# DeltaNet and GELU MLP on one core: beta laid out in its order of use, early loads on two queues, weights that wait for no load, and a new order for every engine

## The chip, the cores and the metric

The kernel runs on one core of one Trainium2 chip. The core has five engines that run side by side: TensorE (PE, with its weight loads as PEld) multiplies matrices, VectorE (DVE), ScalarE (ACT) and GpSimd (POOL) work on tiles, and SyncE (SP) issues transfers. Each runs its own list of instructions in the order in which they stand; semaphores make one wait for another. Transfers between device memory and on-chip memory are issued by SP, ACT and POOL and carried by 16 DMA engines. Products land in PSUM, which has eight banks, and are copied out by ACT or DVE. The metric is the time of one execution on the device, in microseconds.

## The reference

Each of 4 x 8 heads keeps a 48 x 48 state and reads 768 tokens in order; the outputs of all heads then go through a dense layer, a GELU and a second dense layer.

```python
k_n = k / (np.linalg.norm(k, axis=-1, keepdims=True) + 1e-06)
for t in range(S):                                  # S = 768
    kt, vt, bt = (k_n[:, :, t].copy(), v[:, :, t].copy(), beta[:, :, t, None].copy())
    y[:, :, t] = np.einsum('bhd,bhde->bhe', q[:, :, t], state)
    v_old = np.einsum('bhde,bhd->bhe', state, kt)
    state = state + bt[:, :, :, None] * np.einsum('bhd,bhe->bhde', kt, vt - v_old)
...
x = np.ascontiguousarray(attn_out.transpose(0, 2, 1, 3)).reshape(B * S, H * D)   # 3072 x 384
h = x @ w_in                                        # 384 x 2048
g = 0.5 * h * (1.0 + np.tanh(c * (h + 0.044715 * h * h * h)))
return (g @ w_out).astype(np.float32)               # 2048 x 384
```

## The kernel before

The 768 tokens are taken in 12 chunks of 64 (`c`); a chunk has two units (`u = 2c + x`) of 16 heads each. Within a chunk the recurrence is turned into products: a triangular system per head is inverted, and one state goes from chunk to chunk.

The code only declares operations (`A(...)`): the engines on which each may run, what it reads and writes, its PSUM bank. The text table `ORDER` then fixes everything: each word names an operation, its engine (`:a` ACT, `:d` DVE, `:g` POOL, `:s` SP, none for TensorE) and, for products, its bank (`@4`). Every engine runs its words in the order of the table, and `Flow.emit` derives the semaphore waits from what is read and written. Where an operation has alternatives (transposing on TensorE or by DMA, one instruction or two), the table's words choose.

The steps that matter here, with the names used in the table:

- `k0x1.10`, `q2.01`, `v1.00`: loads of a quarter of a chunk's k, q or v (96 KB; chunk 0's k in halves of 48 KB). They stand on SP; chunk 0's k may also stand on ACT. Three chunks' buffers rotate.
- `beta..`: beta is loaded, transposed on TensorE (`betaT`), negated out of PSUM into `bsb` (`betaN`), split into a high and a low part (`betaH`, `betaL`) and spread over rows (`betaS`, `betaC`). Before the change this is done twice, for chunk 0 and for chunks 1 to 11, and all 32 rows are loaded twice, once for each half of a tile.
- `sq`, `sum`, `pow`, `eps`, `inv`: square, sum and root that give 1/norm of k. `kn` (or `knc` for both units) scales k with it; `qb`/`qbc` and `vb`/`vbc` cast q and v.
- `Tk`, `Tq` or `T` transpose a unit's k and q on TensorE, with the evictions `kTk`, `kTq`, `kT`; `turn` does it by a DMA on SP. `GD`, `GQ` or `G` are the products of keys with keys and queries, `dn` and `wq` their evictions (`wqa` with `wqb` on POOL in place of `wq`).
- `F`, `lp`, `x0`, `L`, then `xm1`/`xa1` to `xm6`/`xa6` on DVE, then `xb`: the leaf, which solves blocks of 8 tokens, for a whole chunk. `xe`/`xec` spread its result; `KZ`, `kz`, `GM`, `lw` build the triangular system.
- `X10`/`X11`, `A4`, `rt4`, `B4`, `bde4.` (or `xi4` and `bdc4.`), `A5`, `rt5`, `B5`, `be5.`: the inversion.
- `V`, `K`, `R`, `U`, `Un`, `S`, `Sn`, `Q`, `O`, `On`: the chain over chunks; `On` gives the chunk's output `xo`. `X` with `xT` (TensorE) or `turnx` (DMA) transposes it.
- `up0` to `up15` with `gelu0` to `gelu3`, `down..` with `Z` and `out`: the MLP of a chunk. Its weights come by four loads on POOL: `w1.0`, `w1.1`, `w2.0`, `w2.1`. Before the change `w1.` waits for chunk 1's k and `w2.` for chunk 0's v.
- `fill`: a product of a zero tile with itself into a bank that nobody reads. 140 are declared; the table holds as many as it likes, two before the change.

Of the kernel before, what the change touches and what calls it, by code (L numbers as in the profile page):

```python
# [21 lines left out]
muq1:g ladj4.0:a k2.01:s betaN011:d pow.1:a betaN110:d eps.1:g pad3:d k2.11:s inv.1:d triwq1:d betaN010:d low1:d kn.2:d v0.10:s kn.3:d qb.1:a Tk.2@7
v0.01:s qb.0:g Tk.3@5 kTk.2:d q2.01:s rows1:g Tq.1@4 sq.0a:a betaN111:d kTk.1:d q2.10:s kTq.1:d kTk.3:a sum.0a:d q2.00:s GD.3@4 betaH1:d pow.0a:a
Tq.0@7 sq.2:a eps.0a:d rpad0:g v1.00:s inv.0a:d GD.2@2 betaN000:d GD.1@0 dn.3:a kn.0:g betaL1:d q1.01:s betaH0:d betaS1@6 dn.2:a sum.2:d low2:g
q1.00:s dn.1:a Tk.0@4 first0:d F.1@2 kTq.0:d pow.2:a q1.10:s eps.2:g kTk.0:d trilw2:g q1.11:s GQ.1@0 lp.1:d GD.0@4 betaL0:d x0.1:d L.1@7 q3.01:s
dn.0:a two:d inv.2:d GQ.0@2 wz:d knc.2:g xm1.1:d qbc.2:a F.0@4 k3.00:s wq.0:d xa1.1:d q3.10:s betaS0@5 xm2.1:d xa2.1:d betaS3@2 w1.0:g lp.0:d k3.11:s
betaC0:a xm3.1:d ladj5.1:d L.0@3 triwq2:a ladj4.1:d T.5@4 v0.00:s x0.0:d wqa.1:a xm1.0:d first1:g xa1.0:d kT.5:a qb.3:g xa3.1:d xm2.0:d v0.11:s
xa2.0:d trilw3:g Tq.3@0 xm4.1:d xm3.0:d betaC1:a xa3.0:d qb.2:g xa4.1:d xm5.1:d xm4.0:d T.4@6 xa4.0:d xa5.1:d betaS2@1 xm5.0:d xm6.1:d kT.4:a xa6.1:d
xa5.0:d Tq.2@4 kTq.3:d xb.1:g xm6.0:d triwq5:g xa6.0:d betaC2:a xb.0:d G.5@6 w1.1:g kTq.2:a xe.1:d G.4@0 dn.4:a v2.11:s xe.0:d KZ.1@4 kz.1:a wq.4:d
mwp1:g dn.5:a GM.1@4 xec.1:d KZ.0@0 ladj5.0:a F.2@3 wqa.5:a betaC3:a lw.1:d kz.0:a lp.2:d bdz1:d L.2@3 k3.01:s GM.0@4 x0.2:d X10.1:g KZ.2@6 lw.0:d  # L30
KZ.3@0 kz.3:a X11.1:g kz.2:a xm1.2:d GM.3@0 xa1.2:d rpad1:g A4.1@2 X11.0:g lw.3:d X10.0:g rt4.1:d k3.10:s xm2.2:d A4.0@1 X11.3:g xa2.2:d v1.01:s
B4.1@2 xm3.2:d xa3.2:d rt4.0:d q3.11:s GQ.2@6 GM.2@4 vb.0:a xm4.2:d vb.1:g wq.2:d k4.11:s B4.0@1 bde40.1:a triwq3:g lw.2:d V.0@6 X10.3:g k4.01:s
bde41.1:a bde40.0:a k4.00:s wqb.1:g xa4.2:d A4.3@2 xm5.2:d bde41.0:a A5.1@0 k4.10:s rt4.3:d GQ.3@4 R.0:a rt5.1:d A5.0@1 X11.2:g B4.3@2 v1.10:s rt5.0:d
B5.1@0 bde40.3:a xa5.2:d q3.00:s B5.0@7 X10.2:g xm6.2:d fill115@1 xa6.2:d be50.1:d be50.0:a v1.11:s wq.3:d xb.2:g be51.1:a A4.2@3 sq.3:a w2.0:g
# [224 lines left out]
def bass_deltanet__then__act_gelu_tanh_kernel(  # L259
# [24 lines left out]
    with nc.allow_non_contiguous_dma("strided loads"), nc.allow_low_precision("bf16 pipeline"):  # L284
# [619 lines left out]
```

## Time and profile before

| | us |
|---|---|
| median of 3 runs | 253.88 |
| lowest and highest run | 253.4, 254.34 |
| span of the profiled execution, which is its own time | 254.7 |
| PE busy | 226.0 (89%) |
| DVE busy | 185.8 (73%) |
| ACT busy | 157.4 (62%) |
| POOL busy | 130.1 (51%) |
| moved by DMA | 28.25 MB, mean 111 GB/s |

The page has the busy time of each engine over the span and in 40 slices, and then the chain of work that ended last. A row of the timeline gives start, length, engine, line, operation and tiles, with the count of instructions that were merged, and in brackets the idle time before it and what ended it. Rows of groups give busy time and the mean of one in ns. `PEclk` or "granted clock" is the TensorE clock as a share of full speed. L472 is a load of k, q or v, L824 an up product, L835 a down product.

### The profile page before, as it was taken

The page shows a single profiled execution, that of the slowest core. Times are in us where ns is not written, and L with a number is a line of the kernel's source. Part 1 is how long each engine was busy: PE and PEld are TensorE (multiplying, and loading weights), DVE is VectorE, ACT ScalarE, POOL GpSimd, SP SyncE. Part 2 cuts the span into 40 slices and gives each one's busy share as a digit, 9 for nine tenths or more (in the row PEclk, how much of TensorE's full clock was granted, in tenths as well). Part 3 has the DMA queues.
Part 4 walks back from the last instruction along what each step waited for, and adds up shares of the span by engine and source line. Part 5 has one row for each costly group of instructions (what it writes and reads, how often), then busy time and mean ns, then how long its engine had stood idle before and what let it go on. Part 6 is the DMA issues. An engine that isn't in the chain of part 4 may idle for free.

```text
span 254.7 us, 12256 instructions
## 1 busy us (share of the span) xinstructions
PE 226.0 (89%) x5500; PEld 178.3 (70%) x5502; DVE 185.8 (73%) x445; ACT 157.4 (62%) x244; POOL 130.1 (51%) x159
## 2 busy tenths in 40 slices
PE   0259558899999998999999899999999999999994
PEld 0148347687877877777778778787786778678672
DVE  6599989955996989898888779898494665755100
ACT  2637747949568888967647577743866534436261
POOL 7647448347563397627358968472535525330000
PEclk9999956689999999999999999999999999999999
DMA  5986995987785679789678517787359320332042
GB/s 103 165 144 118 184 162 95 165 127 117 128 130 105 112 126 124 135 165 147 119 146 167 100 36 131 147 153 130 56 93 167 62 49 4 33 68 64 3 93 62
DMA packets 104532, 28.25 MB, mean 111 GB/s; under 512 B 98592, under 2 KB 103712, under 8 KB 104480
## 3 DMA queue, kind: packets, MB, share of 16 engines
q1 hardware_dynamic: 99200, 23.79, 54.0%
q0 software_dynamic: 2880, 3.15, 7.8%
q8 instruction: 43, 0.70, 1.2%
q10 hardware_dynamic: 2400, 0.54, 1.1%
q14 instruction: 9, 0.07, 0.1%
HBM read 20.64 MB, written 4.72 MB: 100 GB/s over the span
## 4 chain that ended last, share of the span: by engine, by line
PE 73%; DVE 15%; ACT 4%; DMA 2%; ACTq 2%; issue 2%; SPq 1%; POOL 0%
PE ps L835 24%; PE ps L824 22%; PE ps L692 5%; PE ps L620 3%; PE ps L752 3%; PE ps L773 2%; DMA vraw<-in_v_dram 2%; PE ps L697 2%; PE ps L564 2%; DVE lw L623 2%; DVE xl L658 2%; PE ps L633 2%; PE ps L759 2%; DVE ps L655 2%; PE ps L609 1%
## 5 line engine op out<-in xcount | busy, mean ns | idle before, releaser
L824 PE MATMUL ps<-xT,W 128*128 128x256 bf16 x576 | 76.8, 277 | 0.4 <-DVE xl L658 0.4
L835 PE MATMUL ps<-W,gT 128*128 128x384 bf16 x384 | 72.7, 326 | 0.0
L828 ACT ACTIVATE gT<-ps 128x1024 bf16<-128x1024 f32 x48 | 48.4, 1022 | 26.4 <-PE ps L824 25.8
L824 PEld LDWEIGHTS ps<-xT,W 128*128 128x128 bf16 x576 | 52.2, 99 | 9.3 <-DVE xl L658 0.5
L835 PEld LDWEIGHTS ps<-W,gT 128*128 128x128 bf16 x384 | 34.0, 97 | 18.2
L682 POOL TENSOR_SCALAR_AFFINE_SELECT bd<-lw 64x512 bf16<-64x512 bf16 x34 | 22.6, 667 | 37.7 <-DVE lw L623 28.6
L704 DVE TENSOR_TENSOR rl<-ps,two 128x384 bf16<-128x384 f32 (+1 forms) x48 | 22.9, 484 | 9.7 <-PE ps L692 9.5
L623 DVE CAST_PREDICATED lw<-mlw,ps 128x832 bf16<-128x832 uint16 x24 | 24.3, 1018 | 6.8 <-PE ps L620 6.5
L499 POOL TENSOR_TENSOR nrm<-nrm,half 128x16 f32<-128x16 f32 x9 | 26.6, 2956 | 2.8 <-DVE nrm L497 2.7
L343 ACT ACTIVATE bd<-ps 32x256 bf16<-32x256 f32 (+1 forms) x40 | 16.8, 428 | 8.2 <-PE ps L692 4.4
L692 PEld LDWEIGHTS ps<-lw,bd 128*128 128x128 bf16 x384 | 15.5, 98 | 4.2 <-POOL bd L682 1.2
L692 PE MATMUL ps<-lw,bd 128*128 128x32 bf16 (+1 forms) x384 | 17.2, 183 | 1.2 <-POOL bd L682 1.1
L658 DVE TENSOR_TENSOR xl<-ps,xl 128x96 bf16<-128x96 f32 (+4 forms) x72 | 16.0, 228 | 2.0
L655 DVE TENSOR_TENSOR ps<-ps,xl 128x64 f32<-128x64 f32 (+5 forms) x72 | 15.6, 221 | 2.0 <-PE ps L649 0.5
L343 ACT ACTIVATE ob<-ps 128x384 f32<-128x384 f32 x17 | 8.3, 490 | 14.0 <-PE ps L835 14.0
L722 POOL COPY bd<-xi 64x256 f32<-64x256 f32 x20 | 8.0, 401 | 16.4 <-ACT xi L343 8.5
L540 PE MATMUL ps<-ident,tok 128*128 128x128 bf16 x80 | 7.8, 246 | 8.1 <-POOL tok L531 3.8
L531 POOL TENSOR_TENSOR tok<-kraw,nrm 128x384 bf16<-128x384 f32 x9 | 8.5, 945 | 12.7 <-DVE bsb L349 5.6
L349 ACT ACTIVATE kT<-ps 128x512 bf16<-128x512 f32 x18 | 10.4, 596 | 6.4 <-PE ps L609 6.4
L343 ACT ACTIVATE dn<-ps 128x512 bf16<-128x512 f32 x18 | 10.4, 593 | 5.3 <-PE ps L564 5.3
L620 PE MATMUL ps<-kT 48*64 48x56 bf16 (+1 forms) x768 | 11.1, 196 | 2.8 <-ACT kT L349 1.4
L599 POOL TENSOR_TENSOR zt<-xb,blk 128x2048 bf16<-128x2048 bf16 x3 | 10.9, 3642 | 4.1 <-DVE xb L669 3.9
(132 smaller groups left out, 428.3 us busy)
## 6 DMA issues: line engine op xcount, KB each, us to landing
qraw<-in_q_dram SPq DMA_DIRECT2D x48, 96.0 KB, 3.6
vraw<-in_v_dram SPq DMA_DIRECT2D x48, 96.0 KB, 3.5
kraw<-in_k_dram SPq DMA_DIRECT2D x44, 96.0 KB, 3.6
out_dram<-ob SPq DMA_DIRECT2D x22, 192.0 KB, 3.0
W<-in_moe_w_in_dram POOLq DMA_DIRECT2D x2, 768.0 KB, 8.8
W<-in_moe_w_out_dram POOLq DMA_DIRECT2D x2, 768.0 KB, 9.6
kraw<-in_k_dram ACTq DMA_DIRECT2D x7, 48.0 KB, 3.3
out_dram<-ob SPq DMA_DIRECT2D x3, 96.0 KB, 2.2
```

Of the source, the lines that this page charges most:

```text
L343: return e.activation(out, in_, ACT.Copy) if e is nc.scalar else e.tensor_copy(out, in_)
L499: if e is nc.scalar else e.tensor_tensor(nr[:, 1, hx], nr[:, 0, hx], half[:, hx], ALU.pow), reads=[nrn, "half"] + ["one"] * (c < ROOTS),
L620: ins = e.matmul(P(ps("GM"))[hf(a), o_ + c0:o_ + c1], kT[s][r, y, g, hf(a)], kT[s][r, z, g, C * a + c0:C * a + c1])
L623: A(("dve",), op("lw"), lambda e, P: e.copy_predicated(lw[m][:, :, 0:LW - LB], mlw[:, :, :].rearrange("p w t -> p (w t)")[:, 16:16 + LW - ...
L655: A(("dve",), f"xm{m}.{c}", lambda e, P, m=m, w=w, part=part: e.tensor_tensor(part(P), P(f"L.{c}")[:, off[m]:off[m] + 2 * H * w].rearrange ...
L658: A(("dve",), f"xa{m}.{c}", lambda e, P, m=m, part=part: e.tensor_tensor(xl[y][:, :, m + 1:LB], part(P), xl[y][:, :, m + 1:LB], ALU.add), ...
L682: A(("pool", "dve"), op(f"X1{a}"), lambda e, P, src=lw[m][hf(a), :, LW - C:LW], dst=bd[b_][hf(a), :, hf(a)], a=a: e.affine_select(out=dst, ...
L692: ins = e.matmul(P(name)[:, C * h + c0:C * h + c1], bd[b_][:, h, :], rhs[:, h, :])
L704: A(("dve",), op(f"rt{i}"), lambda e, P, i=i, c0=c0, c1=c1, r_=r_: e.tensor_tensor(r_[:, 0:H, c0:c1], P(ps(f"A{i}")).rearrange("p (h t) -> ...
L824: ins = e.matmul(P(ph)[:, 256 * f:256 * f + 256].rearrange("p (x t) -> p x t", x=2), W1[:, j, 128 * (i + f):128 * (i + f) + 128], x_[:, :, ...
L828: A(("act",), f"gelu{i // 4}.{c}", lambda e, P, i=i, ph=ph: e.activation(g_[:, i:i + 4, :], P(ph).rearrange("p (f t) -> p f t", f=4), ACT. ...
L835: ins = e.matmul(P(po)[:, 0:DM], g_[:, f, 128 * b:128 * b + 128], W2[:, f, :], start=(f == 0), stop=(f == FC - 1))
```

## The change

Beta's loads now write 16 rows, in the order in which the heads are used, in four loads of 24 KB; one set of transposes serves all chunks, `betaN` is two instructions, `betaH` and `betaL` one each, and `betaS` three groups of four chunks. The loads of chunks 0 to 2 may stand on SP or ACT. The weights' loads read no other load's buffer any more. And the whole table `ORDER` is a new one: 153 operations change engine, four units' transposes (`T.6`, `T.10`, `T.15`, `T.18`) and three chunks' (`X.1`, `X.2`, `X.11`) become DMA transposes, the inversion's `xi4`/`bdc4.` form goes out for `bde4.` everywhere, and 36 zero products stand in it, 16 of them ahead of `betaT` and all ahead of the first up product.

```diff
 ORDER = """
-bdz3:d tmplz:g k0x1.10:a k1.01:s tmpl0:g tmpl1:g bdz5:d k0x1.00:a beta11:s blk1:g one:g pad2:g pad0:d pad5:d ident:g trilw0:d beta01:s beta10:a bdz4:d
...
+k1.01:s pad5:g tmplz:g k0x1.01:a pad3:g tmpl0:g mmlw:g bdz1:g tmpl1:g k0x1.10:s rowz:g ident:d half:d bdz2:d one:d blk1:d identf:d wz:d fill20@0
+fill79@7 fill6@0 fill90@0 fill46@0 ident2:g fill30@0 fill78@2 fill44@0 fill109@0 k0x1.11:a ladj4.1:d k0x1.00:a bdz0:d bdz3:d triwq5:d unit:d blk2:g
...
-        braw = sb("braw", [32, NC, 2, C], F32)
+        braw = sb("braw", [2 * H, NC, 2, C], F32)
...
-            bv = beta.rearrange("b h s -> (b h) s").rearrange("r (c t) -> r c t", t=C)
-            for z, c0, c1 in (("0", 0, 1), ("1", 1, NC)):
+            bv = beta.rearrange("b h s -> (b h) s").rearrange("(m r y) (c t) -> m y r c t", m=2, y=2, t=C)
+            for a in range(2):
                 for y in range(2):
-                    A(("sp", "act"), f"beta{z}{y}", lambda e, P, y=y, c0=c0, c1=c1: e.dma_start(braw[:, c0:c1, y, :], bv[:, c0:c1, :]),
-                      writes=[f"braw{z}{y}"], dma=f"beta{z}{y}")
+                    A(("sp", "act"), f"beta{a}{y}", lambda e, P, a=a, y=y: e.dma_start(
+                        braw[H * y:H * y + H, :, a, :],
+                        bv[a ^ y, y]), writes=["braw"], dma="beta")
...
+            A(PE, "betaT", trans, reads=["braw", "identf"], alloc=("psb", 1), mode="f", mm=2 * NC)
+            for y in range(2):
+                A(("dve",), f"betaN{y}", lambda e, P, y=y: neg(
+                    e, bsb[:, :, :].rearrange("p c (x y g) -> p (c x) y g", x=2, y=2)[:, :, y, :],
+                    P("psb")[:, 0:2 * H * NC].rearrange("p (c y x g) -> p c y x g", y=2, x=2, g=4)[:, :, y, :, :]), writes=[f"bsb{y}"], frees=["psb"])
...
-                            A(("sp", "act") if c == 0 and n == "k" else SP, f"{n}{c}" + ("" if x is None else f"x{x}") + f".{a}{y}",
+                            A(("sp", "act") if c < 3 else SP, f"{n}{c}" + ("" if x is None else f"x{x}") + f".{a}{y}",
...
                 A(("pool",), f"w1.{i}", lambda e, P, f0=f0: e.dma_start(W1[:, :, f0:f0 + FF // 2], w1v[:, :, f0:f0 + FF // 2]),
-                  reads=["kraw10", "kraw11"], writes=[f"W1{i}"], dma=f"w1{i}")
+                  writes=[f"W1{i}"], dma=f"w1{i}")
                 A(("pool",), f"w2.{i}", lambda e, P, n0=n0: e.dma_start(W2[:, n0:n0 + FC // 2, :], w2v[:, n0:n0 + FC // 2, :]),
-                  reads=["vraw00", "vraw01"], writes=[f"W2{i}"], dma=f"w2{i}")
+                  writes=[f"W2{i}"], dma=f"w2{i}")
...
-              reads=[f"xl{y}", f"xl0{y}", f"bc_{0 if c == 0 else 1 if c < 4 else 2 if c < 8 else 3}"], writes=[f"xb{y}"])
+              reads=[f"xl{y}", f"xl0{y}", f"bc_{c // 4}"], writes=[f"xb{y}"])
```

ACT's list at the start of the program, before (`kraw` is a load of k, `braw` of beta, `one` the operation that loads the root's table, `sq` the square of k):

```order
L472 DMA kraw<-in_k_dram 64x4x48 x2
L432 DMA braw<-in_beta_dram 32x11x64
L472 DMA kraw<-in_k_dram 64x4x48
L432 DMA braw<-in_beta_dram 32x64
L472 DMA kraw<-in_k_dram 64x4x48
L343 ACT_TABLE_LOAD
L343 ACTIVATE lw<-tmpl 128x896
L472 DMA kraw<-in_k_dram 64x4x48
L366 ACT_TABLE_LOAD
L366 ACTIVATE one<-one 128x1
L495 ACTIVATE sq<-kraw 128x384
```

And after:

```order
L470 DMA kraw<-in_k_dram 64x4x48 x3
L470 DMA kraw<-in_k_dram 64x8x48 x3
L433 DMA braw<-in_beta_dram 8x12x64
L470 DMA kraw<-in_k_dram 64x8x48
L433 DMA braw<-in_beta_dram 8x12x64
L367 ACT_TABLE_LOAD
L367 ACTIVATE one<-one 128x1
L496 ACTIVATE nrm<-nrm 128x8
L496 ACTIVATE nrm<-nrm 128x16
```

ACT issues nine loads in place of five ahead of its table, the first squares and the copy of the template have gone from it (they stand on DVE and POOL), and one table load is left.

POOL's list around the first load of weights (`W`), before; the `kraw`, `nrm` row is a scaling of k, `xb` the leaf's result:

```order
L531 TENSOR_TENSOR tok<-kraw,nrm 128x8x48
L397 AFFINE_SELECT low<-low 128x1
L501 TENSOR_SCALAR nrm<-nrm 128x16
L411 COPY lw<-tmpl 128x448
L524 TENSOR_TENSOR tok<-kraw,nrm 128x2x8x48
L481 DMA W<-in_moe_w_in_dram 128x3x1024
L400 CAST xl<-unit 128x16
```

And after:

```order
L391 TENSOR_TENSOR own<-blk 128x64
L373 AFFINE_SELECT mlw<-mlw 64x64
L479 DMA W<-in_moe_w_in_dram 128x3x1024
L370 MEMSET muq 128x64
L392 TENSOR_TENSOR sel<-ident,own 128x1024
L412 COPY lw<-tmpl 128x448
L412 COPY wq<-tmpl 128x256
L375 AFFINE_SELECT mlw<-mlw 64x64
L529 TENSOR_TENSOR tok<-kraw,nrm 128x8x48
L383 AFFINE_SELECT rows<-rows 128x1024
L481 DMA W<-in_moe_w_out_dram 128x8x384
L522 TENSOR_TENSOR tok<-kraw,nrm 128x2x8x48
```

The first load of weights now stands ahead of every scaling of k on POOL, and a second one (`w2.1`) ahead of chunk 2's; `sel` has come from DVE to POOL.

TensorE's list in chunk 1 before, with the transposes of the output `xo` between products of the chain (L752, L773) and of the MLP (L824, L835):

```order
L697 MATMUL ps<-bd,rl_1 128x64 x8
L807 MATMUL ps<-ident,xo 128x128 x6
L752 MATMUL ps<-st,kT 64x48 x32
L835 MATMUL ps<-W,gT 128x384 x8
L824 MATMUL ps<-xT,W 128x256 x9
L773 MATMUL ps<-rs,bd 128x48 x16
```

And what stands in SP's list for it after:

```order
L470 DMA kraw<-in_k_dram 64x8x48
L809 DMA_TRANSPOSE xT<-xo 128x6x128
L470 DMA kraw<-in_k_dram 64x8x48
L551 DMA_TRANSPOSE kT<-tok 128x8x128 x4
L844 DMA out_dram<-ob 64x2x384
```

The six products have left TensorE, and the transpose stands on SP among the loads of later chunks, with the transposes of four units' k and q behind it.

More of the change, by code (lines that the diff above doesn't have):

```diff
@@ L22 @@
[L22 to L29, printed above, removed]
@@ new lines, in load_beta, with trans @@
+                    A(("sp", "act"), f"beta{a}{y}", lambda e, P, a=a, y=y: e.dma_start(
+                        braw[H * y:H * y + H, :, a, :],
+                        bv[a ^ y, y]), writes=["braw"], dma="beta")
+            def trans(e, P):
+                for c in range(NC):
+                    ins = e.transpose(P("psb")[:, 2 * H * c:2 * H * c + 2 * H], braw[:, c, :, :].rearrange("r x t -> r (x t)"), identf[:, :])
+                return ins
+            A(PE, "betaT", trans, reads=["braw", "identf"], alloc=("psb", 1), mode="f", mm=2 * NC)
```

212 lines of the change are left out of this document (103 added, 109 removed).

## The prediction

> **What bounds the kernel now.** I read the page first, then the busy time by stretches, then the chain of waits, then the timeline of the stretch that the chain leaves to engines other than TensorE. The stretches (core's time, length, busy time and count of PE, PEld, DVE, ACT, POOL, granted clock, DMA share, GB/s):
>
> ```profile
> 0.00:10.00 10.00, 1.46 (x12) 1.35 (x12) 5.19 (x15) 4.54 (x7) 7.05 (x26) 1.00 0.71 125
> 10.00:20.00 10.00, 4.74 (x90) 3.80 (x91) 9.01 (x24) 4.87 (x11) 5.11 (x9) 1.00 0.86 152
> 20.00:30.00 10.00, 7.19 (x181) 5.92 (x179) 9.59 (x42) 6.95 (x13) 6.50 (x11) 1.00 0.79 138
> 40.00:50.00 10.00, 8.10 (x260) 7.16 (x260) 9.82 (x21) 8.79 (x15) 5.51 (x8) 0.67 0.92 139
> 60.00:240.00 180.00, 177.32 (x4491) 138.91 (x4488) 136.66 (x313) 115.47 (x176) 94.97 (x93) 1.00 0.60 105
> ```
>
> Two stages show. From 60 to 240 us TensorE has work in 177.3 of 180 us, at full clock, with VectorE at 76% and the DMA engines at 60%: products set the pace, and only fewer products or an earlier start can shorten it. In the first 50 us VectorE is the full one (9.0 to 9.8 of 10) and TensorE waits. That opening ends where the first product with the MLP's weights starts:
>
> ```profile
> 8.46 0.51 ACT L495 ACTIVATE sq<-kraw 128x384 f32<-128x384 f32 x1
> 10.56 0.95 DVE L497 TENSOR_REDUCE nrm<-sq 128x16 f32<-128x768 f32 x1 [0.30 <-ACT sq L495]
> 22.14 0.24 DVE L655 TENSOR_TENSOR ps<-ps,xl 128x96 f32<-128x96 f32 x1
> 29.13 0.29 DVE L669 TENSOR_TENSOR xb<-xl,bc 128x128 bf16<-128x128 bf16 x1
> 46.67 0.81 ACT L343 ACTIVATE xo<-ps 128x768 bf16<-128x768 f32 x1
> 49.94 3.81 PE L824 MATMUL ps<-xT,W 128*128 128x256 bf16 x18
> ```
>
> So: norms start at 8.46, the leaf solves at 22.14, xb of chunk 0 is done at 29.4, its output xo at 47.5, and the first up product starts at 49.9. The rest takes 254.7 - 49.9 = 204.8 us. The sum is made against the profiled execution's 254.7 us; the runs' median of 253.88 lies 0.8 under it, which comes off at the end.
>
> **Term 1: norms to xb of chunk 0.** The rows that the work there is priced by:
>
> ```profile
> 13.06 1.96 DVE L531 TENSOR_TENSOR tok<-kraw,nrm 128x384 bf16<-128x384 f32 x1
> 14.95 0.54 DVE L531 TENSOR_TENSOR tok<-kraw,nrm 128x384 bf16<-128x384 f32 x1
> 12.63 2.05 POOL L382 TENSOR_SCALAR_AFFINE_SELECT rows<-rows 128x1024 bf16<-128x1024 bf16 x1
> 9.00 0.55 DVE L497 TENSOR_REDUCE nrm<-sq 128x8 f32<-128x384 f32 x1 [1.40 <-ACT sq L495]
> 9.70 0.83 ACT L495 ACTIVATE sq<-kraw 128x768 f32<-128x768 f32 x1
> L421 DVE MEMSET bd<- 128x512 f32 x4 | 1.9, 485 | 1.1 <-PEq L889 1.0
> 4.80 1.28 ACT L343 ACT_TABLE_LOAD   x1 [4.80 <-issue]
> 0.80 1.39 ACTq L472 DMA_DIRECT2D kraw<-in_k_dram  x2
> kraw<-in_k_dram ACTq DMA_DIRECT2D x7, 48.0 KB, 3.3
> ```
>
> Before, the first square stands on ACT behind a table load, a copy and a second table load, until 8.46. Now it stands on DVE, and its last piece of k is ACT's third issue: 0.80 + 3 x 0.70 = 2.9, and 3.3 more to land, 6.2. DVE has three memsets of 0.49 and a dozen shorter operations before that, some 4.6 us by my count from its start at 1, so it is free in time. Then DVE's own list: square 0.5 (as ACT's 0.51), copy 0.5, sums 0.55 and 0.95, the square of chunk 1's k 0.9 (as ACT's 0.83): 9.6. ACT has issued nine loads by 0.8 + 9 x 0.66 = 6.7 and loaded its table by 8.2, so the roots cost 0.3; four small operations 0.8, two scalings 2 x 0.54: 11.8. Chunk 0's first half: sum 0.55, copies and roots 1.5, scaling 0.54: 14.4. Then 0.3 + 0.95 + 0.28 for beta's high part, chunk 2's sum and lp, 1.1 for x0 and small ones: 17.0. Fewer beta copies (2 for 8, of 0.1 to 0.25 each) are in this.
>
> The leaf: from 22.14 to 29.1 DVE did 24 steps and 2.4 us of other work between, so the steps take 4.5; now they have 0.8 among them: 22.3, and with xb 0.3 22.6, against 29.4. That is 6.8 us earlier if nothing waits. Against it: the 1.96 row is the same scaling that takes 0.54 in the next, and it lies almost wholly beside POOL's 2.05 us select, so POOL's work can hold DVE up. POOL now has sel near those scalings and rows1 near betaL; I take one such stop, 1.4, off: 5.4 us earlier. Bounds: 6.8 and, with three stops, 2.6. One new wait stands in ACT's list: the square of chunk 2's k waits for its fourth load with five evictions and a root queued behind it, and DVE's sum and lp behind those. That load is SP's eleventh, out by 0.8 + 11 x 0.67 = 8.2 and 3.6 later landed (row below), 11.8; ACT gets there near 12.4, so 0.6 us covers it.
>
> **Term 2: xb to the first up product.** 46.67 + 0.81 - 29.42 = 18.1 us from xb to xo. In the new order ACT is the longest list here: 12 evictions of kT, wq, bd or bc, 4 of the short corner kind, 2 scaled ones, 6 wide ones.
>
> ```profile
> L349 ACT ACTIVATE kT<-ps 128x512 bf16<-128x512 f32 x18 | 10.4, 596 | 6.4 <-PE ps L609 6.4
> L343 ACT ACTIVATE bd<-ps 32x256 bf16<-32x256 f32 (+1 forms) x40 | 16.8, 428 | 8.2 <-PE ps L692 4.4 <-PE ps L697 3.1
> L346 ACT ACTIVATE bd<-ps,low 128x512 bf16<-128x512 f32 x8 | 5.4, 672 | 0.0
> L343 ACT ACTIVATE us<-ps 128x768 bf16<-128x768 f32 x10 | 8.1, 809 | 3.2 <-PE ps L773 3.1
> ```
>
> 12 x 0.596 + 4 x 0.428 + 2 x 0.672 + 6 x 0.81 = 15.1, plus 1.1 from xb to its first eviction: 16.2, or 1.9 earlier when ACT never waits. I take 0.9, bounds 1.9 and -1. The 36 zero products (2 before) all stand ahead of the first up product; 16 of them ahead of beta's transposes. A product of 512 columns is priced from 384 columns below, 5.21 / 32 = 0.163, so 0.22, and 0.43 where the clock is half: the 16 take 6.9 us from some 3 us on, and nothing on PE is due before 11.8. The 20 others cost 4.4 to 8.6 if nothing covered them; most stand behind a product that waits for an eviction of 0.6 anyway, and I take 0.3 (bounds 0 and 4.4).
>
> ```profile
> 245.98 5.21 PE ps L835 x32
> 241.07 4.91 PE ps L824 x45
> 50.01 3.74 PE ps L824 x18
> 33.00:43.00 10.00, 7.53 (x255) 6.78 (x256) 8.97 (x24) 5.20 (x10) 7.29 (x12) 0.50 0.68 117
> 46.50:53.00 6.50, 6.09 (x133) 4.87 (x120) 5.05 (x8) 5.61 (x9) 3.56 (x2) 0.51 1.26 190
> ```
>
> **Term 3: the weights' loads.** They now wait for no load: w1.0 stands on POOL behind some 7 us of templates (19 operations of 0.1 to 0.65), w2.1 behind rows1, near 17 us, both by my count. Before, w1.0 went out at 23.45. What a load of weights does to its neighbours:
>
> ```profile
> kraw<-in_k_dram SPq DMA_DIRECT2D x44, 96.0 KB, 3.6
> 23.45 1.01 POOL L481 DMA_DIRECT2D W<-in_moe_w_in_dram  x1
> 25.57 2.83 SPq L472 DMA_DIRECT2D kraw<-in_k_dram  x1
> 29.16 2.57 SPq L472 DMA_DIRECT2D qraw<-in_q_dram  x1
> W<-in_moe_w_in_dram POOLq DMA_DIRECT2D x2, 768.0 KB, 8.8
> 6.00:8.00 2.00, 1.42 (x12) 1.29 (x12) 0.62 (x4) 1.97 (x3) 1.93 (x7) 1.00 0.96 165
> 190.51 4.84 DMA vraw<-in_v_dram
> ```
>
> While w1.0 moved, SP's issue, else 0.64 to 0.68, took 2.83 and 2.57: three loads in 6.2 us, where nine fit, so some 4.1 us lost for all behind it. SP's 29th load (the last of chunk 1's q) would go out at 0.8 + 29 x 0.67 = 20; with two loads of weights ahead 28, landed at 32. ACT casts that q near 26.5, and POOL the v of chunk 0 near 25. So up to 5 us of waiting; with w2.1 coming too late to matter, 1. I take 2.5, since w2.1 moves for about half the time that matters. Also the gain of two queues is small: the share is 0.96 at 165 GB/s at 6 us, with SP alone on most of it. [...]
>
> Opening: 5.4 + 0.9 - 0.3 - 2.5 = 3.5 us earlier. Up starts at 46.4.
>
> **Term 4: products removed.** Four units' transposes (T, 8 products each) and three chunks' (X, 6 each) go to SP's queue; all of them stand after up's start in the order before.
>
> ```profile
> 79.44 0.45 PE ps L540 x8
> 55.79 2.46 SPq L553 DMA_TRANSPOSE kT<-tok  x1
> ```
>
> 4 x 0.45 + 3 x 6 x 0.056 = 2.8 us less on the engine that sets the pace. Their evictions go too, off the path. SP carries 29 transposes for 22, each 1.2 to 2.5 us of issue; queued behind a waiting transpose are loads of q, k and v for two chunks on. Everything else after up's start is the same products in another order, with DVE, ACT and POOL lists no longer than before: 0, bounds -3 (all of the 2.7 idle in 60 to 240 recovered) and +6 (one more detour like the 4.84 above, where the chain leaves PE for a late v).
>
> Sum: 254.7 - 3.5 - 2.8 = 248.4; less 0.8: **247.6**, say 247.5.
>
> **Rivals.** (a) The opening does better: no load waits and no port stops, the zero products keep the clock up, so that the half clock at 46.5 to 53 goes too. 18 up products took 3.74 there and take 18 x 4.91 / 45 = 1.96: 1.8 us. 6.8 + 1.9 + 1.8 + 2.8 off: 241.4 - 0.8 = 240.6. For it: the leaf's end at 22.6 rests on measured steps. Against it: only eight zero products stand between the first KZ and up, so TensorE stays as sparse there as at 33 to 43, where the clock was half. [...] (b) The change does not bring the opening forward, since the loads, not the order, set it: only term 4 stays, 251.1. (c) Both first loads of weights stand fully in the path: -5.0 and a second late load of 4.1 against 6.0: up starts 3.1 later, 254.7 + 3.1 - 2.8 - 0.8 = 254.2, no change. (d) Slower: SP's queue, with seven more transposes that wait, delivers v or q late in the product stage. Each such wait costs 4.84 by the one row above; the gain of 6.3 is gone at the second (1.3 of them), and at two 257.3. Against it: that row stands once in 200 us with 22 transposes.
>
> **Chances.** Forecast 0.48, (a) 0.18, (b) 0.14, (c) 0.09, (d) 0.11. Half a per cent (1.3 us) is about what a measurement of this kernel tells from none. Faster: 0.48 + 0.18 + 0.14 = 0.80; (c) gives 0.07 same and 0.02 slower; slower 0.13. The range leaves out (d) and a part of (a): 241 to 254.5; the forecast's own is 244 to 250.
>
> **What would show it.** xb of chunk 0 near 24 us; ACT's cast of chunk 1's q waiting for a DMA near 27; the first up product at 44 to 49; SP issues of 2 us and more between 9 and 26; from there 200 to 203 us to the end. An up start later than 51, or a PE idle of over 8 us after it, makes the forecast wrong.

## The result: 8.5% slower

The changed kernel takes 276.4 us (median of 4 runs, 275.5 to 277.1), the kernel before 254.1 in the same session; the ratio is 1.085, with a 95% interval of 1.079 to 1.090. The forecast was 247.5. Some executions of a kernel are 1.5% or more slower than its fastest; the ratios in this text leave these out, the medians do not, and the profiles of the third and last row of experiment 4's table and of experiment 6 are of such executions. The profiled execution spans 273.7 us for 254.7, so 19.0 us have to be found. The medians are 22.3 apart: a run's time lies some 1.8 us above its span, and the profiled execution of the kernel before was a long one, for seven later runs of it span 251.6 to 253.6 us. The 3.3 us between 19.0 and 22.3 have no place in the account that follows.

First the busy time by stretches of the changed kernel, with the columns of the prediction (length, busy time and count of PE, PEld, DVE, ACT, POOL, then granted clock, DMA share, GB/s):

```profile
0.00:10.00 10.00, 6.00 (x16) 2.08 (x16) 6.42 (x20) 1.70 (x3) 8.94 (x26) 1.00 0.90 123
10.00:20.00 10.00, 6.74 (x105) 4.71 (x106) 9.05 (x21) 4.96 (x12) 6.75 (x7) 0.66 1.09 172
20.00:30.00 10.00, 6.45 (x141) 4.62 (x136) 7.77 (x36) 6.77 (x12) 6.26 (x12) 0.93 1.13 181
40.00:50.00 10.00, 7.30 (x208) 6.22 (x207) 6.83 (x19) 7.67 (x15) 6.74 (x7) 0.71 0.96 151
60.00:240.00 180.00, 164.49 (x4153) 128.18 (x4151) 135.14 (x295) 111.16 (x176) 91.28 (x82) 0.98 0.59 105
```

From 60 to 240 us TensorE now has work in 164.5 of 180 us, where it had 177.3. From 20 us on no engine of the opening is full any more: VectorE has 7.8 of ten from 20 to 30 and 6.8 from 40 to 50, where it had 9.6 and 9.8. Something makes all of them wait.

The landmarks of the opening, from the timeline of the changed kernel (DVE, ACT, PE, and then the loads that SP and POOL issue):

```profile
6.53 0.61 DVE L494 TENSOR_TENSOR sq<-kraw 128x384 f32<-128x384 f32 x1 [1.04 <-DMA kraw<-in_k_dram]
8.45 3.48 DVE L494 TENSOR_TENSOR sq<-kraw 128x768 f32<-128x768 f32 x1 [0.53 <-DMA kraw<-in_k_dram]
25.67 0.29 DVE L666 TENSOR_TENSOR xb<-xl,bc 128x128 bf16<-128x128 bf16 x1
48.78 0.82 ACT L344 ACTIVATE xo<-ps 128x768 bf16<-128x768 f32 x1
52.13 1.49 PE L821 MATMUL ps<-xT,W 128*128 128x256 bf16 x12
...
8.69 1.92 POOL L392 TENSOR_TENSOR sel<-ident,own 128x1024 bf16<-128x1024 bf16 x1
7.55 1.01 POOL L479 DMA_DIRECT2D W<-in_moe_w_in_dram  x1
17.18 0.94 POOL L481 DMA_DIRECT2D W<-in_moe_w_out_dram  x1
9.32 5.37 SPq L470 DMA_DIRECT2D qraw<-in_q_dram  x3
15.95 3.35 SPq L470 DMA_DIRECT2D qraw<-in_q_dram  x5
```

xb of chunk 0 is done at 25.96 instead of 29.42, 3.5 earlier; the first up product comes at 52.1 instead of 49.9, 2.2 later. From the first up product to the end the two executions compare so (one row each; first the kernel before, then after):

```profile
49.90:254.70 204.80, 198.61 (x4720) 154.92 (x4712) 143.27 (x327) 126.91 (x191) 101.13 (x97) 0.99 0.59 104
```

```profile
52.10:273.70 221.60, 200.04 (x4650) 155.01 (x4646) 147.25 (x316) 129.16 (x200) 94.36 (x85) 0.98 0.54 97
```

The product stage is 221.6 us for 204.8, 16.8 longer, and TensorE idles in 21.6 us of it for 6.2. So 15.4 of the 16.8 are idle time of TensorE. What it waits for, from the waits of the changed kernel between 52 and 274 us (total, times, longest):

```profile
PE ps L792 <- issue: 6.0, 3, 2.6
PE ps L562 <- DMA kT<-tok: 2.5, 4, 1.2
PE ps L618 <- ACT gT L825: 2.4, 1, 2.4
PE ps L618 <- issue: 2.1, 4, 1.2
PE ps L562 <- issue: 1.3, 1, 1.3
PE ps L689 <- DVE bd L681: 0.9, 1, 0.9
PE ps L821 <- DMA xT<-xo: 0.8, 1, 0.8
```

The largest part, 9.4 us, is "issue": TensorE waits for nothing that the profile shows. The same view of the kernel before has 0.9 us of it:

```profile
PE ps L620 <- issue: 0.7, 1, 0.7
PE ps L795 <- issue: 0.2, 1, 0.2
```

Where these pauses stand gives them away. Here is the longest, in TensorE's timeline of the changed kernel:

```profile
231.51 0.27 PE L618 MATMUL ps<-kT 48*64 48x48 bf16 x10 [0.33 <-issue]
231.60 0.44 PE L779 MATMUL ps<-us,tok 64*64 64x48 bf16 x32
231.85 0.46 PE L749 MATMUL ps<-st,kT 48*64 48x48 bf16 x32
232.15 0.58 PE L618 MATMUL ps<-kT 48*64 48x56 bf16 x32
232.56 0.38 PE L792 MATMUL ps<-us,wq 64*64 64x48 bf16 x22
235.51 0.27 PE L792 MATMUL ps<-us,wq 64*64 64x48 bf16 x10 [2.57 <-issue]
```

Both pauses fall into the middle of a group of 32 products that wait for nothing among themselves, and between the two stand 10 + 32 + 32 + 32 + 22 = 128 products, that is 256 instructions, since each product has its weight load. The page shows what comes in such pieces (queue, packets, MB, share):

```profile
q8 instruction: 43, 0.70, 1.1%
```

43 transfers of 16 KB for TensorE's 10,933 instructions (5,463 products and 5,470 weight loads on the page), one per 254. In the trace one of them starts at 232.62, so TensorE went on 2.9 us after its start. The nine pauses of this kind over 0.4 us in the changed kernel stand multiples of 256 apart, within four, when TensorE's weight loads, products and waits for semaphores are counted, and each ends 2.3 to 3.1 us behind the start of such a transfer. The 256 instructions from 231.51 on were through in 1.4 us. The theory that follows, called F: TensorE gets its own instructions in blocks of 256, a block takes some 3.5 us to follow another (the author's estimate from this trace), and where short products go through a block faster, TensorE waits. Its rivals: the pauses belong to the order of the work or to data transfers, and the loss lies in the opening.

### The profile page after: what moved, and what is told of

Same layout as the page of the kernel before. It is cut to its first block, busy times and chain, and to the rows that moved or that the text cites. A ratio compares the mean times of both kernels' runs of the same rounds, so it can differ in the third digit from the quotient of the medians.

```text
span 273.7 us, 12149 instructions
## 1 busy us (share of the span) xinstructions
PE 236.4 (86%) x5463; PEld 180.9 (66%) x5470; DVE 184.4 (67%) x423; ACT 158.6 (58%) x253; POOL 130.6 (48%) x149
## 4 chain that ended last, share of the span: by engine, by line
PE 56%; DVE 12%; SPq 10%; DMA 8%; issue 7%; ACT 5%; POOL 0%; POOLq 0%
PE ps L832 18%; PE ps L821 17%; SPq L470 8%; PE ps L689 4%; DMA kT<-tok 4%; DMA qraw<-in_q_dram 3%; PE ps L618 3%; PE ps L562 2%; PE ps L749 2%; PE ps L792 2%; PE ps L607 1%; PE ps L770 1%; DVE xl L655 1%; DVE ps L652 1%; PE ps L694 1%
## 5 line engine op out<-in xcount | busy, mean ns | idle before, releaser
L821 PE MATMUL ps<-xT,W 128*128 128x256 bf16 x576 | 74.4, 278 | 1.1 <-DMA xT<-xo 0.8
L344 ACT ACTIVATE bd<-ps 32x256 bf16<-32x256 f32 (+1 forms) x56 | 24.8, 446 | 22.7 <-PE ps L694 13.0
L679 POOL TENSOR_SCALAR_AFFINE_SELECT bd<-lw 64x512 bf16<-64x512 bf16 x32 | 21.7, 677 | 33.2 <-DVE lw L621 27.8
L522 POOL TENSOR_TENSOR tok<-kraw,nrm 128x768 bf16<-128x768 f32 x6 | 10.3, 1722 | 15.8 <-DVE nrm L501 8.1
L618 PE MATMUL ps<-kT 48*64 48x56 bf16 (+1 forms) x768 | 12.4, 199 | 6.3 <-issue 3.9
L655 DVE TENSOR_TENSOR xl<-ps,xl 128x96 bf16<-128x96 f32 (+5 forms) x72 | 16.1, 228 | 1.8
L652 DVE TENSOR_TENSOR ps<-ps,xl 128x64 f32<-128x64 f32 (+4 forms) x72 | 15.6, 221 | 2.5 <-PE ps L646 1.1
L584 POOL TENSOR_TENSOR wq<-wq,muq 128x512 bf16<-128x512 bf16 x14 | 16.6, 1187 | 0.3
L344 DVE COPY ob<-ps 128x384 f32<-128x384 f32 x7 | 3.8, 553 | 17.6 <-PE ps L832 17.6
L618 PEld LDWEIGHTS ps<-kT 48*64 48x64 bf16 x768 | 9.9, 117 | 7.7 <-issue 7.2
L562 PE MATMUL ps<-kT 48*64 48x128 bf16 (+1 forms) x448 | 11.0, 219 | 4.6 <-DMA kT<-tok 2.5
```

The source lines that it names most:

```text
L344: return e.activation(out, in_, ACT.Copy) if e is nc.scalar else e.tensor_copy(out, in_)
L618: ins = e.matmul(P(ps("GM"))[hf(a), o_ + c0:o_ + c1], kT[s][r, y, g, hf(a)], kT[s][r, z, g, C * a + c0:C * a + c1])
L655: A(("dve",), f"xa{m}.{c}", lambda e, P, m=m, part=part: e.tensor_tensor(xl[y][:, :, m + 1:LB], part(P), xl[y][:, :, m + 1:LB], ALU.add), ...
L679: A(("pool", "dve"), op(f"X1{a}"), lambda e, P, src=lw[m][hf(a), :, LW - C:LW], dst=bd[b_][hf(a), :, hf(a)], a=a: e.affine_select(out=dst, ...
L821: ins = e.matmul(P(ph)[:, 256 * f:256 * f + 256].rearrange("p (x t) -> p x t", x=2), W1[:, j, 128 * (i + f):128 * (i + f) + 128], x_[:, :, ...
```

## Experiment 1: the same work, blocks shifted

The kernel before gets 19 groups of 4 short products ahead of everything else, in time in which TensorE is idle; they read a constant and nobody reads them.

```diff
+                def four(e, P, n=n):
+                    for p, a in quad:
+                        ins = e.matmul(P(n)[hf(p), 512 * a:512 * a + 8], tmpl[hf(a), 0:C], tmpl[hf(a), 0:8])
+                    return ins
 ORDER = """
-bdz3:d tmplz:g k0x1.10:a k1.01:s tmpl0:g tmpl1:g bdz5:d
+bdz3:d tmplz:g k0x1.10:a k1.01:s tmpl0:g tmpl1:g tick0@6 tick1@6
...
+tick18@6 bdz5:d
```

> The kernel before with 19 x 4 products of 64 x 64 by 8 columns of constants put ahead of all others, in the first 10 us when TensorE has nothing else; nothing reads them. Theory F (TensorE waits for its own instructions): in the trace of after, all long pauses in which TensorE waits for nothing shown stand 256 TensorE instructions apart or a multiple of it, 2.3 to 2.9 us behind the start of a 16 KB instruction transfer, and only where the 256 instructions ahead went by in under about 3.5 us. The added 152 instructions move every such place by 152. By the shortest product times of the trace, 15 blocks of 256 instructions then need less than 3.5 us for 8 before, 12.4 us short in all for 5.7; part of that is hidden by other waits. Expected 2 to 4 us more than before (256 to 258), issue at 3 to 4% of the chain for 2. Rival R (the pauses come from the order of the work or from data transfers): no change within 0.5 us, since the added products lie in idle time.

Measured: 263.3 us (259.4 to 264.3), ratio 1.025 (1.016 to 1.035); the profiled execution spans 260.8 for 254.7. Three pauses have appeared in TensorE's timeline, and they alone:

```profile
52.50 0.28 PE L620 MATMUL ps<-zt,tok 64*64 64x64 bf16 x11 [3.10 <-issue]
70.72 1.15 PE L846 MATMUL ps<-W,gT 128*128 128x384 bf16 x6 [1.86 <-issue]
99.95 0.19 PE L620 MATMUL ps<-zt,tok 64*64 64x64 bf16 x1 [1.55 <-issue]
```

They make 6.5 us, against the 6.1 by which this span is longer; the 0.7 at 140.5 us in the kernel before is gone. The first up product already comes 2.8 us later, at 52.7. So a shift of 152 instructions costs 2.5% with the same products, loads and evictions. Rival R, no change, is out; theory F holds, and its estimate of 2 to 4 us was too small. It also says what the kernel before is: an order whose blocks happen to stand well.

## Experiment 2: the price by itself

The kernel before with 160 such groups ahead of everything, 1280 instructions in a row.

```diff
-            for i in range(19):
+            for i in range(160):
```

> The kernel before with 160 x 4 products of 64 x 64 by 8 columns ahead of all others, 1280 TensorE instructions one behind the other with no wait among them; the time of the whole means nothing here. Theory F: they cannot go faster than 256 in about 3.5 us, 17 to 18 us in all, with a pause of 1 us or more at every 256th and a 16 KB instruction transfer 2.3 to 2.9 us ahead of each pause's end. Rival R: at the 13 ns of a short product that the trace of after shows (32 in 0.42 us), 640 take 8.4 us without a pause.

TensorE's timeline of the first 21 us (one execution):

```profile
1.98 3.35 PE L444 MATMUL ps<-tmpl 64*64 64x8 bf16 x223 [1.98 <-POOL tmpl L368]
7.41 2.14 PE L444 MATMUL ps<-tmpl 64*64 64x8 bf16 x128 [2.07 <-issue]
11.68 1.88 PE L444 MATMUL ps<-tmpl 64*64 64x8 bf16 x128 [2.14 <-issue]
15.96 1.88 PE L444 MATMUL ps<-tmpl 64*64 64x8 bf16 x128 [2.40 <-issue]
20.24 0.60 PE L444 MATMUL ps<-tmpl 64*64 64x8 bf16 x33 [2.40 <-issue]
```

128 products each time, then a pause of 2.1 to 2.4 us. Three blocks take 20.24 - 7.41 = 12.83 us, 4.28 each, so the limit is worse than the 3.5 of the theory. The rival's 8.4 us without a pause is out. The first 446 instructions ran through; the first such transfer of this run starts at 4.90, and TensorE went on at 7.41.

The length of a block alone does not give every pause. The blocks ahead of the two pauses at 39.0 and 45.8 us of the changed kernel took 4.4 and 5.7 us, and TensorE still waited 1.8 and 1.0: there the transfer began 3.6 and 4.3 us behind the first instruction of the block, where ahead of the seven later pauses it began 0.8 to 2.1 us behind it, and block and pause together took 3.4 to 4.3. What sets a transfer off is not shown.

## Experiment 3: which part carries the loss

Two kernels are put together at the first up product of chunk 0: up to there the words of one order, and from there those of the other that are left.

```text
first:  the words of after up to up4.0, then those of before that are left
second: the words of before up to up4.0, then those of after that are left
```

> The opening of after (all words up to the first up product of chunk 0), then all that is left in the order of before. Theory P (the loss lies in the new order of the product stage): 254 to 258, since the opening of after ends 2.2 us later and the rest takes before's 204.8 less a little for what the opening has already done. Rival O (the loss lies in the opening, its loads and zero products, and is carried on through the stage): over 268. Theory F adds: 7 blocks short by 4.4 us, all but two ahead of or at the first up products, so the stage has issue pauses of under 1 us.

> The opening of before with its loads of weights as before, and beta in its new layout, up to the first up product of chunk 0; then all that is left in the order of after. Theory P: 268 to 276, the first up product near 50 and some 220 us from there. Rival O: 252 to 257. Theory F adds: 17 blocks short of 3.5 us by 16.8 us, issue at 5 to 8% of the chain.

Measured: the first 261.6 us, ratio 1.026 (1.021 to 1.031); the second 281.0, ratio 1.104 (1.098 to 1.111). From the first up product to the end, first kernel, then second:

```profile
54.90:258.70 203.80, 197.40 (x4665) 153.36 (x4663) 142.03 (x323) 124.44 (x188) 99.53 (x97) 0.99 0.55 97
```

```profile
61.30:279.50 218.20, 197.87 (x4621) 153.49 (x4614) 142.66 (x310) 126.81 (x195) 87.35 (x80) 0.98 0.56 98
```

Before's order of the product stage takes its 204 us behind either opening, after's 218 to 222 behind either. So the stage's order carries 14 to 17 us, and rival O is out. Both totals lie above what was expected, since the up products start later in both, at 54.9 and 61.3: 4.8 us of pauses at block ends stand ahead of them in the first, and in both the seam leaves work ahead of the up products that each order alone had placed elsewhere.

## Experiment 4: the new order with its blocks elsewhere

The changed kernel with 14, then 22 groups as in experiment 1, and without its zero products and with 23 groups. (A fourth of this kind, with 9 groups, stands in experiment 5.)

```diff
 ORDER = """
-... tmpl1:g k0x1.10:s ...
+... tmpl1:g tick0@6 tick1@6 ... k0x1.10:s ...
```

> The kernel after with 14 x 4 such products ahead of all others, 112 instructions. Theory F: the pauses leave their places (behind O.1, in GM.8, S.5, GM.18, O.10) and come back at others (GM.7, GM.13, O.6, K.8, GM.23); sum of what blocks are short of 3.5 us 14.6 for 15.5, so 274 to 277, the sum hardly changed but no pause at an old place. Rival R: the pauses stay where they are, behind the same products, 276.4 within 0.5.

> The kernel after with 22 x 4 products of 8 columns ahead of all others, 176 instructions, the shift for which the trace of after makes the product stage shortest of instructions (9.9 us of pauses by a rate of 256 in 3.5 us, where it makes 6.9 without a shift and 9.2 were measured). If the pauses add in full: a stage of 224 to 226 us for 221.6. If other waits take half of them: 222.5 to 224. If they cost nothing in this order: 221 to 222.

> The kernel after without zero products and with 23 x 4 products of 8 columns ahead of all others, so that the blocks of the product stage stand 112 instructions further on, the shift for which the trace of after makes the fewest pauses (4.6 us by the same rate for 6.9). Stage of 216 to 218.5 us if pauses add in full, 218 to 221 if not.

| kernel | us, ratio (interval) | up start | stage | pauses of 0.3 us and more at block ends in the stage |
|---|---|---|---|---|
| before | 254.1 | 49.9 | 204.8 | 0.7 |
| after | 276.4, 1.085 (1.079 to 1.090) | 52.1 | 221.6 | 9.2 |
| 112 instructions more | 276.1, 1.073 (1.063 to 1.082) | 56.2 | 220.0 | 5.3 |
| 176 more | 274.1, 1.072 (1.063 to 1.081) | 52.5 | 215.8 | 6.1 |
| no zero products, blocks of after | 273.8, 1.077 (1.069 to 1.084) | 52.0 | 218.1 | 4.7 |
| the same, 112 more | 277.8, 1.083 (1.072 to 1.094) | 55.2 | 221.3 | 5.5 |

In the three shifted kernels the pauses left their old places, and where the blocks stand as in after the pauses stayed there (132.4, 157.8 and 233.5 us for 133.8, 158.5 and 235.5), as F has it. The forecasts of their sizes failed: for 176 instructions 9.9 us of pauses and a stage of at least 221 were expected, and 6.1 and 215.8 came; for the last row 4.6 and a stage of at most 221, and 5.5 and 221.3 came. The place of a block's end can be worked out from the order, but how fast the block ahead of it goes depends on all other waits. The new order has 4.7 to 9.2 us of pauses wherever its blocks stand, and with them taken off in full its stage would still take 210 to 216 us for before's 204. The stages do not follow the pauses: with 6.1 us the stage takes 215.8, with 4.7 it takes 218.1. The runs of one such kernel also lie up to 2.4% apart (270.2 to 276.5 for the fourth row). So the pauses of this order are shown, and that they cost in full is shown in before's order (experiment 1) but not in this one.

## Experiment 5: the opening

The changed kernel with the weights' loads at about the times of before; and without zero products, with 9 groups of short products that keep the blocks of the stage in place.

```diff
-... mln0:g w1.0:g mmuq:g ... rows1:g L.1@2 w2.1:g ... xb.1:g w2.0:g ... triwq3:g w1.1:g
+... knc.2:g w1.0:g ... xb.1:g w1.1:g ... wqb.1:g w2.0:g w2.1:g
```

```diff
-... wz:d fill20@0 fill79@7 fill6@0 ...
+... wz:d ...
```

> The kernel after with the four loads of weights at about the times of before (behind the scaling of chunk 2's k, behind xb of chunk 1, and behind the masks of chunk 1). Theory W (early weights hold up the loads of q and v): SP's issues between 9 and 24 us fall back to 0.65 us, chunk 0's q is cast 3 to 4 us earlier than 27.8, and the first up product comes at 48 to 50; total 272 to 275. Rival (ACT and the instruction pauses set the opening): up start 51 to 53, total 276 within 1.

> The kernel after without its 36 zero products of 512 columns; 9 x 4 products of 8 columns ahead of all others keep the count of instructions, and so the blocks of the product stage, where they were. Theory Z0 (they were covered by waits): up start within 1 us of 52.1, 276 within 1.5. Rival Z1 (they lie in the path of the opening): up start 2 to 4 us earlier, 272 to 274. Rival Z2 (they hold the clock up): the granted clock from 10 to 50 us falls further below 0.7 and the opening gets 1 to 3 us longer.

With late weights the three loads of q that took SP 5.37 us to issue take 2.10, and the five that took 3.35 still take 3.35:

```profile
9.69 2.10 SPq L470 DMA_DIRECT2D qraw<-in_q_dram  x3
12.51 3.35 SPq L470 DMA_DIRECT2D qraw<-in_q_dram  x5
```

Five in 3.35 is the usual 0.67 each. So the first load of weights held up the three loads of q; behind the second one, issued at 17.18, two loads of v took 2.73 us and two of q 3.34, where without it each pair takes 1.31. Chunk 0's q is cast at 25.8 instead of 27.8, 2 us earlier and not 3 to 4. The first up product comes at 50.1, 2.0 earlier, yet the whole takes 278.0 us, ratio 1.089 (1.081 to 1.098), outside theory W's 272 to 275: the stage is 227.0, and more than takes back the gain.

Without the zero products up starts at 52.0 as with them; they are covered. Of the clock the rows say 1.00 from 10 to 20 us without them and 0.66 with them, and from 30 to 40 us 0.67 in both. The row without them (the one with them is the second row of the first table of the result):

```profile
10.00:20.00 10.00, 5.55 (x88) 4.35 (x92) 9.10 (x20) 4.63 (x11) 7.02 (x7) 1.00 1.22 178
```

This 1.00 is not a measured clock: the trace without zero products has no record of the clock before 21.7 us, the one with them none before 8.2, and the view shows 1.00 until the first. The products tell it. Four transposes, twice with zero products (recorded at full clock from 18.4 us and at half at 14.3) and once without them:

```profile
18.77 0.39 PE L538 MATMUL ps<-ident,tok 128*128 128x128 bf16 x4
14.31 0.61 PE L538 MATMUL ps<-ident,tok 128*128 128x128 bf16 x4 [0.78 <-DVE tok L529]
18.46 0.61 PE L546 MATMUL ps<-ident,tok 128*128 128x128 bf16 x4 [0.69 <-DVE tok L537]
```

So without them TensorE was still at half clock at 18.46 us, by the 0.61; with them it has the full clock from 8.2 to 11.6 and again from 18.4 to 28.7. Rival Z1 is out; of rival Z2 the lower clock came, and the 1 to 3 us that it was to cost did not.

One more kernel joins the changed opening with late weights to before's stage and 27 groups of short products for the blocks.

> The opening of after with its loads of weights at about the times of before, then the product stage in the order of before, and 27 x 4 products of 8 columns ahead of all others, which put the blocks of 256 instructions where the fewest are short (6, by 3.9 us in all, 3 of them ahead of the first up product). Theory F with P: up start 48 to 50, then 203.5 to 205: 251.5 to 254. Rival O2 (the new opening brings nothing whatever stands behind it): up start 51 to 53, 255 to 258.

It takes 264.1 us, ratio 1.041 (1.036 to 1.047), a miss: the output of chunk 0 is there at 47.4, but the first up product starts at 59.4. In the chain of this kernel stands why:

```profile
44.71 11.46 DMA qraw<-in_q_dram
```

The second half of the weights, now at 43 us, meets the loads of chunk 3's q, and a cast of that q stands on DVE ahead of work for the first chunks. Early weights cost the loads of chunk 0, late ones those of chunk 3.

## Experiment 6: the product stage

Three edits of the changed kernel: the seven transposes back on TensorE (the one shown); ten transposes of SP's queue ahead of the loads that were issued while they could have gone; and 88 groups of up and down products pulled forward in TensorE's list, to break up the runs of short products.

```diff
-... turn.6:s ... turnx.1:s ... turn.10:s ... turnx.2:s ... turn.15:s ... turn.18:s ... turnx.11:s ...
+... T.6@0 kT.6:d ... X.1@4 xT.1:d ... T.10@6 kT.10:d ... X.2@2 xT.2:a ... T.15@1 kT.15:d ... T.18@6 kT.18:d ... X.11@7 xT.11:a ...
```

> The kernel after with the seven transposes that the change gave to SP's queue (kT of four units, xT of three chunks) back on TensorE, at the same places, with the evictions that they had before. Theory D (transposes in SP's queue land late): the two waits of 5.3 us for kT in the chain go and SP issues the loads behind them earlier; 2.8 us of products come back: 270 to 274. Rival (the transposes were hidden): 2.8 us and seven evictions more, 278 to 280. Theory F alone: 14 blocks short by 13.9 us for 16 by 15.5, no change within 2 us.

> The kernel after with ten transposes of SP's queue moved ahead of the loads that were issued while their input was already there (in the trace of after one for xT waited 10.4 us behind such loads, another 14.9, one for kT 5.8); TensorE's list is that of after. Theory Q (transposes stand behind loads in SP's queue, and TensorE waits for them): kT and SP leave the chain of the product stage in part, 270 to 274. Rival (the loads that now come later cost as much): 276 to 279.

> The kernel after, with 88 groups of up and down products pulled forward in TensorE's list behind the first up product, so that runs of short products are broken up; the other engines' lists, the products and the loads are as in after. Theory F: the blocks of 256 instructions are short of 3.5 us by 9.2 in all (by product times) for 15.5, 4.3 of the 9.2 ahead of the first up product: 269 to 273, issue in the chain under 5% for 7. Rival P2 (the stage loses by evictions and transfers that come late for the new order, not by instruction fetches): the pulled products only push the short ones back, 276 to 279.

Measured: transposes on TensorE 285.9 us, ratio 1.114 (1.105 to 1.124); transposes first 273.2, 1.067 (1.057 to 1.077); products pulled forward 320.8, 1.250 (1.239 to 1.261). The stage of the last:

```profile
53.30:320.40 267.10, 221.43 (x4648) 162.83 (x4646) 145.77 (x316) 129.48 (x200) 93.60 (x85) 0.90 0.44 81
```

No pause of 0.3 us at a block's end is left in that stage, where F still expected blocks short by 4.9 us, and TensorE idles in 45.7 us of it for 21.6, while its products take 221.4 us for 200.0 at a clock of 0.90 for 0.98. So the pauses are gone and the kernel is 44 us slower, far outside both expectations. TensorE's longest waits there are for ACT's gelu (4.7 us) and for DVE's `rt` (3.1) and `X10`, `X11` (2.9). That fits a simple reading: each product pulled forward pushes back a short one for which ACT and DVE, and through them the next chunk, wait. The short products of this order would then be its critical chain, which would also be why a pause among them costs; no run shows this by itself.

Moved back to TensorE, the seven transposes cost 9.5 us by the medians (7.5 by the ratios), and not the 2.8 of their products. The blocks move too, by 100 instructions, but the pauses in that stage are 7.6 us for 9.2 and do not explain it. Theory D is out, the DMA transposes help this order.

Putting transposes first in SP's queue takes the whole from 276.4 to 273.2, 3.2 us by the medians and 4.5 by the ratios, which lies in theory Q's 270 to 274. How it does so is not shown: the waits for kT go from 2.5 us to 1.9 only, the pauses at block ends from 9.2 to 8.0, and the profiled execution, the longest of the four runs, has a stage of 221.1 for 221.6. Late transposes are at most a fifth of the 22.3 us.

## Experiment 7: beta alone

The kernel before with the new layout of beta and nothing else; 4 groups of short products replace the 32 instructions of the spread that falls away.

```diff
-... betaT1@0 ... betaT0@6 ... betaS0@5 ... betaS1@6 ... betaS2@1 ... betaS3@2 ...
+... tick0@6 tick1@6 tick2@6 tick3@6 ... betaT@6 ... betaS0@5 ... betaS1@1 ... betaS2@2 ...
```

> The kernel before with the new layout of beta alone (4 loads, 12 transposes into 16 columns, 2 copies, 3 spreads in place of 4), all other words where they were, weights waiting for the loads as before. The spread that falls away is 32 TensorE instructions, and 4 x 4 products of 8 columns ahead of all others put them back, so the blocks of 256 are those of before (8 short of 3.5 us, by 5.7). Expected of the beta part by itself: 253 to 254.5, no change. Rival (the copies and the smaller transposes bring the opening forward): up start at 48 to 49.5, 252.5 to 253.5. Against theory F: a change of more than 1.5 us with the blocks in place.

It takes 253.7 us (10 runs), ratio 0.999 (0.996 to 1.002): no change. Up starts at 49.9 as before. With the blocks in place the profiled execution has no pause over 0.3 us at a block's end, where before has one of 0.73. This is the nearest that a kernel of this study came to the one before; none beats it.

## Why the prediction was wrong, step by step

The forecast for the profiled execution was 248.4; it came out at 273.7. Of these 25.3 us, 5.7 are in the opening and 19.6 in the stage. The 0.8 taken off at the end took before's 254.7 for a usual span; it was a long one.

- **Term 1, norms to xb, 5.4 us earlier: 3.5.** Inside its bounds of 6.8 and 2.6. The mis-sized piece is the square of chunk 1's k on DVE, taken as 0.9 by ACT's row: it took 3.48, beside POOL's product `sel` of 1.92 and its copies. The two later squares of this form on DVE took (5.7 - 3.48) / 2 = 1.1 each by the group's row. "One stop of 1.4" was taken off, and the one that came was 2.6.

```profile
L494 DVE TENSOR_TENSOR sq<-kraw 128x768 f32<-128x768 f32 x3 | 5.7, 1885 | 0.6 <-DMA kraw<-in_k_dram 0.5
```

  The trace shows this square at three times the 1.1 us of the later ones, beside POOL's work. That POOL's work holds DVE up is the author's estimate: no run here took it away. In eight kernels with this opening (changed kernel, experiments 3 to 6) the square took 2.9 to 4.3 us beside `sel` and the copies, in the two with late weights 3.5 and 2.9, so the load of weights is not the reason.
- **Terms 2 and 3, xb to the first up product: 5.7 us longer instead of 0.9 shorter less 0.3 and 2.5.** Term 3 had the right size: experiment 5 puts the early weights at 2.0 us of up start for the 2.5 taken. The zero products cost nothing, for 0.3 taken. Of the rest, 3.4 us are three pauses at block ends between 37 and 50 us (1.79, 1.04 and 0.54); what they cost there is not shown, since without zero products one pause of 2.55 stands in that stretch and up starts at the same time. Term 2 counted ACT's evictions and had no line for TensorE's instructions.
- **Term 4, products removed, 2.8 us less.** The sign was right and the size too small in this order: undone, it costs 7.5 to 9.5.
- **"Everything else after up's start is the same products in another order: 0, bounds -3 and +6."** This is the step that failed. The stage came out 19.6 over the forecast of it, 204.8 - 2.8, and experiment 3 puts 14 to 17 us on its order alone. Nor were the other lists no longer: in the stage DVE is busy 147.3 us for 143.3 and ACT 129.2 for 126.9. TensorE idles 15.4 us more: 8.5 at the ends of instruction blocks (9.4 - 0.9) and 6.9 mostly in waits for transposes, evictions and gelu. The other 4.2 are products that take longer: the granted clock is 0.78 from 52 to 60 us, where before had 0.83 from 49.9 to 60, and 0.83 and 0.85 in the stretches around two of the long pauses, where it had 1.00. By their busy time that is 2.5 us (0.17 of 8.34 and 0.15 of 7.10); the remainder was not traced.

```profile
52.10:60.00 7.90, 5.52 (x116) 4.64 (x113) 4.24 (x9) 4.27 (x7) 3.07 (x4) 0.78 0.72 136
70.00:80.00 10.00, 8.34 (x272) 5.62 (x261) 6.99 (x16) 5.68 (x13) 7.48 (x10) 0.83 0.69 125
230.00:240.00 10.00, 7.10 (x198) 5.01 (x194) 4.61 (x7) 2.00 (x3) 2.07 (x3) 0.85 0.28 51
```

- **Rival (d), slower by late transposes in SP's queue, 257.3.** The right side with the wrong weight: 0.11, and the waits for kT and xT are 3.3 of the 15.4. The profile of before has a trace of the other part: 0.73 us of "issue" in the middle of a group of products, and 43 instruction transfers on the page. The prediction says nothing of either.
- **Rival (a), the clock.** The prediction's rows say 1.00 over the first 30 us. Before 22.7 us the trace of the kernel before has no record of the clock, and the products show half: four transposes before and after that time took

```profile
11.21 0.61 PE L540 MATMUL ps<-ident,tok 128*128 128x128 bf16 x4 [3.79 <-POOL tok L531]
27.17 0.39 PE L540 MATMUL ps<-ident,tok 128*128 128x128 bf16 x4
```

  In the changed kernel the 16 zero products at the start take 6.0 us from 3.37 on, and the clock was full from 8.2 to 11.6 us and half until 18.4. From 46.5 to 53 us, where the rival had the half clock gone, it was 0.79 for before's 0.51. What the rival calls port stops are stops of DVE beside POOL's work, as under term 1; that a port is their cause is not shown.
- **What was said to show it.** xb of chunk 0 came at 26.0 and not near 24. SP's slow issues between 9 and 26 us came. The wait for q near 27 came, on POOL and for chunk 0, one load landing 9.0 us after its issue. Up at 52.1 was beyond the 51, and TensorE's idle time beyond the 8 us, that were to make the forecast wrong.

What stays open: how much of the 8.5 us the new order would lose to other waits if the pauses were gone, and which link of its chain between ACT, DVE and TensorE makes up the 6.9.

## What to carry to other kernels

The order of a list is not free even where no engine has much more to do: here that of the product stage alone was worth 14 to 17 us (experiment 3). Count TensorE's instructions in blocks of 256, and look for blocks whose products are shorter than some 4 us in all (experiment 2 took 4.28 a block; in the changed kernel seven of nine pauses stood behind such blocks, two behind longer ones). Long products pulled in between short ones took away every pause of 0.3 us and more at a block's end in the stage, and the kernel was 44 us slower (experiment 6): look first at who waits for the short ones. Where a profile has "issue" in the middle of a group that waits for nothing, look for the distance in instructions between two of them. And before judging an edit on such a kernel, put back the number of instructions that it removed or added ahead of the rest: 152 instructions that nobody needed were worth 2.5% here.

## What was not expected of the hardware

TensorE's instructions come in transfers of 16 KB during the run: 43 in the changed kernel for 10,933 instructions, one per 254, with its nine pauses over 0.4 us multiples of 256 instructions apart, within four. Behind these and the one such pause of the kernel before, TensorE went on 2.2 to 3.1 us after a transfer began, and in a run of short products a block took 4.28 us with its pause (experiment 2), where the short products of 64 rows by 8 columns need 1.9 us for one. The first 446 instructions of that run went through without a pause; how many TensorE holds at a time is not shown.
